# A fused attention and expert kernel: where the first routing runs, how token rows are turned, and when they are fetched

## The chip, the cores and the metric

The kernel runs on one core of one Trainium2 chip. A core has a matrix engine (TensorE, PE in the profile), a vector engine (VectorE, DVE), an activation engine (ScalarE, ACT), a general engine (GpSimd, POOL) and an engine that only issues transfers (SyncE, SP). They run side by side and wait for each other through semaphores. On-chip memory is SBUF, with 128 partitions; matmul results land in PSUM, eight banks of 512 fp32 columns in each partition. The metric is the device time in microseconds (us), the median of several runs.

## The reference: what is computed

Two stages. The first is attention with random features, over 8 batches, 8 heads, 576 positions, head dimension 64, 128 features:

```python
proj = np.einsum('bhsd,md->bhsm', x, omega)            # x is q or k
phi  = np.concatenate([np.cos(proj), np.sin(proj)], -1) / np.sqrt(m)
kv   = np.einsum('bhsm,bhsd->bhmd', k_p, v)
z    = np.sum(k_p, axis=2)
out  = (q_p @ kv) / (q_p @ z)
```

The result, as 4608 token rows of 512, goes through a mixture of 8 experts. Each token takes the one expert whose embedding has the largest cosine with the row; the gate is the softmax weight of that expert (temperature 0.1):

```python
expert_idx = np.argmax(xn @ en.T / tau, axis=1)
out[mask]  = gate_w[mask, None] * (np.maximum(x[mask] @ w1[e], 0) @ w2[e])
```

with w1 of 512 x 1024 and w2 of 1024 x 512 for each expert.

## The kernel before

**Attention.** There are 32 steps, one for each batch and pair of heads (heads i and i+4). The order of the instructions is written by hand (`manual_schedule`), as a software pipeline: pass n of the loop at L940 works on step n's keys and queries, on the projection of step n+1's keys, on the numerators of step n-1, and on the squares of steps n-2 and n-3. On PE a pass runs, in this order: `proj_q(n)` (L225, L232), `kv_turn(n-1)` (L308, L316), `proj_k(n+1)` (L213), `num(n-1)` (L341, 72 records), the transposes of raw k and q (`turns`, L180), `kv_products(n)` (L287). VectorE copies kv results out of PSUM (`kv_copy` L297, `kv_out` L326), takes the fraction of the angle (`frac`, L249), its absolute value for the cosine (`fold`, L255), the normalised output (`norm`, L356 to L358), and the sums of squares (L385). It also copies the turned keys, 640 columns, out of PSUM (`copy_k`, L191). ScalarE rounds the angles (`whole_turns`, L245), takes four sines a step (`wave`, L262), squares rows (L377) and copies the turned queries, 512 columns (`copy_q`, L200). GpSimd sums the key features for the denominator (`zsum`, L273 to L277, five additions for each of the two halves), casts the output to fp16 rows (L373), adds the logits (L407), and issues the cast loads of the expert weights (L92, L98).

The numerators wait for `kv_out`, which on VectorE stands behind whatever was put ahead of it in the pass; and `kv_turn` waits for `zsum`.

**Routing.** Tokens are sorted by expert into blocks of 128 rows, each of a single expert, so that a block is one dense product. The first half of the batches is routed during attention (`route_first`, passes 18 on): `choose` finds the expert of each token, `scan` and `rank` (two matmuls) its position within the expert, `places` and `places2` the block and row, `block_hot`, `row_hot` and `invert` the inverse: for each row of a block, its token. Only whole blocks of the first half are placed there; the first K1 = 11 blocks are safe to fetch before the second half is known. The rest is routed by `route_second`, during the first blocks of the expert stage. The gate needs the root of the sum of squares: Newton steps on VectorE for the first half (L693 to L716), `pow` on GpSimd for the second (L690).

**Experts.** The number of blocks is fixed: NBLK = 4608/128 + 8 - 1 = 43, the most that any split of the tokens can need. A block beyond those in use holds token numbers out of bounds, which gather and scatter skip. In iteration j PE runs `hidden(j+1)` (L840: 32 matmuls, weights stationary), the transposes of block j+2's rows (`turn_x`, L798: four of 128 x 128 in fp16, then a copy from PSUM at L792 or L790) and `result(j)` (L861: 8 matmuls of 512 columns). The rows are fetched with an indirect transfer into a ring of three buffers (`gather`, L759), five blocks ahead from iteration 0 on. The scaled result goes out with an indirect transfer (L874). The weights sit in SBUF, and the expert of a block is read into a PE register (`expert_of`); 40 further registers hold the addresses of its weight tiles (`place`).

Of the kernel before, what the change touches and what calls it, by code (L numbers as in the profile page):

```python
# [28 lines left out]
def kernel(  # L29
# [43 lines left out]

    ident = persist.tile([P, P], FP32)
    ident16 = persist.tile([P, P], FP16)
    sltb = persist.tile([P, P], BF16)
    onesb = persist.tile([P, P], BF16)

    w1_sb = persist.tile([P, E, 4, 1024], FP16)
    w2_sb = persist.tile([P, E, 8, 512], FP16)  # L80
# [5 lines left out]
    W1BASE, W2BASE = 18046, 83328  # L86
# [28 lines left out]
    eblk = persist.tile([1, NBLK], I32)  # L115
# [3 lines left out]
    io_k = io_p[:, 0:NBLK]  # L119
    io_kf = persist.tile([1, NBLK], FP32)  # L120
    pref = persist.tile([P, E], BF16)
    tri = persist.tile([P, E, E], FP32)
    sm = persist.tile([P, 12, E], FP32)
    zmask = persist.tile([P, 2], FP32)
    pio2 = persist.tile([P, 1], FP32)
    sel = persist.tile([P, SG, E], BF16)
    pm = persist.tile([P, SG], BF16)
# [4 lines left out]
    with tc.tile_pool(name="psA", bufs=1, space=PSUM) as psA, tc.tile_pool(  # L132
# [6 lines left out]

        steps = [(b, i) for b in range(B) for i in range(NPAIR)]  # L140
# [5 lines left out]
        def load(n, t, src):  # L146
            b, i = steps[n]
            for hh in range(2):
                nc.sync.dma_start(
                    out=t[64 * hh : 64 * hh + 64],  # L150
                    in_=src[b, i + 4 * hh].rearrange("(p c) d -> p c d", c=NCH),
                )

        raw = {}


        def load_kq(m):
            if m == -2:
                raw[m] = w1_sb[:, E - 2].rearrange("p c f -> p (c f)").bitcast(FP32)[:, 0 : NCH * 64]
                load(0, raw[m].rearrange("p (c d) -> p c d", d=64), k)  # L160
                return
            t = pa.tile([P, 2 * NCH, 64], FP32, tag="kq", name="kq", bufs=1)
            load(min(m + 2, NS - 1), t[:, 0:NCH], k)
            if m + 1 >= 0:
                load(m + 1, t[:, NCH:], q)
# [22 lines left out]
        def copy_k(m):  # L188
            t = pa.tile([P, 5 * P], FP32, tag="kT", name="kT", bufs=1)
            if m + 1 >= 0:  # L190
                nc.vector.tensor_copy(t, qreg[:, 0 : 5 * P])  # L191
                st.setdefault(m + 1, {})["t"] = t
            else:
                nc.vector.tensor_copy(t[:, 0 : 4 * P], qreg[:, 0 : 4 * P])  # L194
                nc.vector.tensor_copy(t[0:64, 4 * P :], qreg[0:64, 4 * P : 5 * P])
            st.setdefault(m + 2, {})["kT"] = t

        def copy_q(m):
            t = pa.tile([P, 4 * P], FP32, tag="qT", name="qT", bufs=1)
            nc.scalar.activation(t, qreg[:, 5 * P :], AF.Copy)  # L200
            st[m + 1]["qT"] = t

# [4 lines left out]
        def proj_k(n):  # L207
            t = st[n]["kT"]
            for j in range(5):
                for par in range(2 if j < 4 else 1):  # L210
# [4 lines left out]
                        lhsT=t[r0 : r0 + 64, j * P : j * P + P],  # L215
# [5 lines left out]
        def proj_q(n):  # L221
            d = st[n]
            for par in range(2):
# [4 lines left out]
                    rhs=d["qT"][r0 : r0 + 64],  # L228
                    start=True,
                    stop=True,  # L230
                )
            nc.tensor.matmul(  # L232
                qreg[:, 1024:1152],
                lhsT=omT[64:P],
                rhs=d["t"][64:P, 4 * P :],
# [30 lines left out]
        def zsum(n, half):  # L266
# [5 lines left out]
            zt = pa.tile([P, 2, P], FP32, tag="zt", name="zt", bufs=1)  # L272
            nc.gpsimd.tensor_tensor(zt, t[:, 0:2], t[:, 2:4], ALU.add)  # L273
            nc.gpsimd.tensor_tensor(zt, zt, t[:, 4:6], ALU.add)  # L274
            nc.gpsimd.tensor_tensor(zt, zt, t[:, 6:8], ALU.add)  # L275
# [73 lines left out]
        def norm(n):  # L349
# [3 lines left out]
            rd = pa.tile([P, 2, 5], FP32, tag="rd", name="rd")  # L353
# [15 lines left out]
        def to_rows(n):  # L369
# [3 lines left out]
            nc.gpsimd.tensor_copy(xrow[b, i // 2][:, :, i % 2], st[n]["xa"][:, 0:NCH, 0:64])  # L373

        def squares(n):
            x = st[n]["xa"][:, 0:NCH, 0:64]
            nc.scalar.activation(x, x, AF.Square)  # L377
# [11 lines left out]
        def square_rows(g):  # L389
            s0 = g * SG  # L390
            for par in range(2):
# [3 lines left out]
                nc.vector.tensor_copy(t[here, :, NPAIR:], t[there, :, 0:NPAIR])  # L395
                nc.vector.tensor_reduce(
# [3 lines left out]
        def sums(n):  # L400
            b, i = steps[n]
            src = st[n]["xa"][:, 0:NCH, 64 : 64 + E]
            if i == 0:
                lacc[b] = pa.tile([P, NCH, E], FP32, tag="la", name="la", bufs=3)
# [24 lines left out]
        emb_n = persist.tile([P, 2], FP32)  # L429
        load_kq(-2)  # L430
        for a in range(2):
            nc.scalar.dma_start(out=om2[:, a], in_=omega[:])
        nc.scalar.dma_start(out=emb, in_=moe_expert_emb[:])
        load_kq(-1)
        load_v(0)
        make_identity(nc, ident)
        nc.vector.memset(zmask, 0.0)
        nc.vector.memset(pio2, PI_2)
        nc.vector.memset(zmask[0:64, 0:1], 1.0)
# [15 lines left out]
        nc.gpsimd.memset(keep[:, :, 0:1], 0.0)  # L455
        nc.scalar.activation(
            emb2[:, :, 0], emb.rearrange("p (h d) -> p h d", d=64), AF.Square, accum_out=emb_n[:E, 0:1]
        )
        nc.scalar.activation(emb_n[:E, 0:1], emb_n[:E, 0:1], AF.Sqrt)
        nc.scalar.preload_act_table_set("silu_and_others")  # L460
        nc.vector.memset(nm2[:, 1, 4 * W : 5 * W], 1.0)
        tp_om = kreg[:, 0:P]
# [3 lines left out]
        copy_k(-2)  # L466
        proj_k(0)
# [9 lines left out]
        frac(0, "k")  # L477
        copy_k(-1)
        copy_q(-1)
        load_kq(0)  # L480
        tp_e = ps[:, 6 * 512 : 6 * 512 + H * E]
        for h in range(H):
# [4 lines left out]
            )  # L487

# [41 lines left out]
        def choose(g):  # L530
# [4 lines left out]
            nc.vector.tensor_copy(l0, a0[64:P])  # L535
            nc.vector.tensor_copy(l1, a1[0:64])
            nc.vector.tensor_tensor(l0, l0, a0[0:64], ALU.add)
            nc.vector.tensor_tensor(l1, l1, a1[64:P], ALU.add)
            mx = lmax[:, s0 : s0 + SG]
            nc.vector.tensor_reduce(mx, lg, axis=AX.X, op=ALU.max)  # L540
            nc.vector.tensor_tensor(sel, lg, bc(mx, [P, SG, E], 2), ALU.is_equal)
            nc.vector.tensor_tensor(sel, sel, bc(pref, [P, SG, E], 1), ALU.mult)
# [594 lines left out]
```

## Time and profile before

| | us |
|---|---|
| median of 3 runs | 520.08 |
| lowest and highest | 517.64, 525.76 |
| span of the profiled execution | 527.1 |

| group (line) | count | busy us | mean ns |
|---|---|---|---|
| first expert product, PE (L840) | 1376 | 83.7 | 219 |
| second expert product, PE (L861) | 344 | 81.3 | 379 |
| numerators, PE (L341) | 2304 | 160.9 | 235 |
| transposes of token rows, PE (L798) | 172 | 16.8 | 219 |
| copy of turned keys, VectorE (L191) | 32 | 26.3 | 821 |
| copy of turned queries, ScalarE (L200) | 32 | 19.1 | 598 |
| copy of turned token rows, VectorE (L792) | 35 | 14.8 | 424 |
| `choose`, last operation, VectorE (L544) | 4 | 2.6 | 662 |

Matmuls are pipelined, so the mean of one is its latency and not the time it adds. The first matmuls of the expert stage start at 340.25 us, so the stages take roughly two thirds and one third of the span.

### The profile page before, as it was taken

What the parts mean: (1) busy time and instruction counts of PE and PEld (TensorE: products, weight loads), DVE (VectorE), ACT (ScalarE), POOL (GpSimd) and SP (SyncE); (2) the same over time, 40 slices, a digit from 0 to 9 for tenths busy, and PEclk for the clock granted to TensorE, in tenths of its full rate; (3) what the DMA queues carried; (4) which work ended last, traced back from release to release, by engine and by line L of the source; (5) the groups of instructions that cost most, each with busy time, mean ns of one, the idle gap of its engine ahead of it and who ended that gap; (6) DMA issues with size and microseconds to landing.
All of it is one profiled execution on the core that took longest, in us unless ns stands there. A gap on an engine that the chain in (4) does not pass through costs nothing.

```text
span 527.1 us, 18983 instructions
## 1 busy us (share of the span) xinstructions
PE 480.5 (91%) x8012; PEld 397.2 (75%) x8012; DVE 353.1 (67%) x634; ACT 318.1 (60%) x375; POOL 377.8 (72%) x529
## 2 busy tenths in 40 slices
PE   5899999889999989999997989778989999999993
PEld 4798888779888878888886878666757776767771
DVE  4588787798788799999799899569613323232320
ACT  4678878676887885886686767644533332323331
POOL 2689999796999897989987688864545455554532
PEclk9799999999999999999899899999999999999998
DMA  4467778866698786687686774543223222223110
GB/s 114 120 149 160 170 161 176 162 132 132 158 183 149 167 173 132 154 176 146 129 186 119 156 137 100 106 95 82 91 92 106 97 68 103 95 93 104 56 52 0
DMA packets 57891, 65.61 MB, mean 124 GB/s; under 512 B 29637, under 2 KB 37829, under 8 KB 57808
## 3 DMA queue, kind: packets, MB, share of 16 engines
q0 software_dynamic: 18304, 30.97, 28.8%
q1 hardware_dynamic: 39200, 33.36, 25.4%
q8 instruction: 64, 1.05, 0.8%
q14 instruction: 19, 0.16, 0.1%
q10 hardware_dynamic: 304, 0.08, 0.1%
HBM read 67.90 MB, written 16.01 MB: 159 GB/s over the span
## 4 chain that ended last, share of the span: by engine, by line
PE 45%; POOL 21%; DVE 15%; ACT 8%; issue 7%; DMA 1%; POOLq 0%; ACTq 0%; SPq 0%; DVEq 0%
PE ps L840 12%; PE ps L861 10%; PE ps L341 8%; PE ps L287 4%; PE ps L180 4%; POOL zt L273 4%; POOL zs L276 3%; POOL zt L275 3%; POOL zt L274 3%; PE ps L213 3%; POOL zs L277 3%; PE ps L798 2%; ACT siq L245 2%; DVE cok L255 2%; ACT sik L262 2%
## 5 line engine op out<-in xcount | busy, mean ns | idle before, releaser
L840 PEld LDWEIGHTS <-w_sb 128*128 x1376 | 80.2, 98 | 21.0 <-issue 15.4
L341 PE MATMUL ps<-kv,siq 128*64 128x73 f32 x1152 | 81.1, 236 | 15.0 <-DVE kv L326 14.3
L840 PE MATMUL ps<-kq,w_sb 128*128 128x128 f16 x1376 | 83.7, 219 | 6.3 <-ACT kq L790 3.4
L852 DVE TENSOR_SCALAR cok<-ps 128x512 f16<-128x512 f32 x34 | 23.5, 692 | 88.1 <-PE ps L798 61.5
L341 PEld LDWEIGHTS ps<-kv,siq 128*64 128x64 f32 x1152 | 67.2, 142 | 19.5 <-ACT sik L245 8.1
L861 PE MATMUL ps<-w_sb,cok 128*128 x344 | 81.3, 379 | 0.1
L341 PE MATMUL ps<-kv,coq 128*64 128x73 f32 x1152 | 79.8, 233 | 0.0
L341 PEld LDWEIGHTS ps<-kv,coq 128*64 128x64 f32 x1152 | 67.8, 143 | 0.0
L200 ACT ACTIVATE qT<-ps 128x512 f32<-128x512 f32 x32 | 19.1, 598 | 68.2 <-DVE kT L191 64.6
L759 POOL DMA_INDIRECT xin_all<-rf_x,prm x43 | 46.7, 1086 | 15.1 <-issue 7.0
L861 PEld LDWEIGHTS <-cok 128*128 128x128 f16 x344 | 31.9, 98 | 31.0 <-issue 0.5
L249 DVE SCALAR_TENSOR_TENSOR sik<-sik,ps 128x1152 f32<-128x1152 f32 x32 | 43.2, 1350 | 6.7 <-ACT sik L245 6.7
L874 POOL DMA_INDIRECT out_dram<-sik,prm x22 | 22.1, 1006 | 35.2 <-ACT sik L873 35.0
L213 PE MATMUL ps<-omT,kT 64*128 64x128 f32 x576 | 46.2, 292 | 0.6 <-DVE kT L194 0.6
L273 POOL TENSOR_TENSOR zt<-sik 128x256 f32<-128x256 f32 x32 | 23.9, 747 | 31.8 <-ACT sik L262 31.5
L874 POOL DMA_INDIRECT out_dram<-siq,prm x21 | 21.6, 1026 | 34.4 <-ACT siq L873 32.6
L276 POOL TENSOR_TENSOR zs<-zt 128x128 f32<-128x128 f32 x64 | 41.4, 646 | 5.0
L249 DVE SCALAR_TENSOR_TENSOR siq<-siq,ps 128x1152 f32<-128x1152 f32 x32 | 43.0, 1344 | 2.2 <-ACT siq L245 2.1
L213 PEld LDWEIGHTS ps<-omT,kT 64*128 64x128 f32 x576 | 40.1, 196 | 2.1 <-DVE kT L194 1.0
L873 ACT ACTIVATE sik<-ps,gpos 128x512 f32<-128x512 f32 x22 | 15.1, 688 | 43.6 <-PE ps L861 43.6
L180 PE MATMUL ps<-ident,kq 128*128 128x128 f32 x288 | 40.2, 287 | 0.9 <-DVE siq L249 0.9
L245 ACT ACTIVATE sik<-ps 128x1152 f32<-128x1152 f32 x32 | 36.2, 1131 | 7.6 <-PE ps L213 7.2
(220 smaller groups left out, 1263.2 us busy)
## 6 DMA issues: line engine op xcount, KB each, us to landing
w_sb<-in_moe_w_dram POOLq DMA_DIRECT2D x32, 512.0 KB
kq<-in_k_dram SPq DMA_DIRECT2D x64, 144.0 KB, 3.4
kq<-in_q_dram SPq DMA_DIRECT2D x64, 144.0 KB, 3.4
v<-in_v_dram SPq DMA_DIRECT2D x34, 144.0 KB, 2.9
rf_x<-xb SPq DMA_DIRECT2D x32, 144.0 KB, 7.4
xin_all<-in_v_dram SPq DMA_DIRECT2D x30, 144.0 KB, 3.3
xin_all<-rf_x,prm POOLq DMA_INDIRECT x43
out_dram<-sik,prm POOLq DMA_INDIRECT x22
```

The costliest lines, as they stand in the source:

```text
L180: nc.tensor.transpose(qreg[:, j * P : j * P + P], t[:, j * P : j * P + P], ident)
L213: nc.tensor.matmul(kreg[:, s * P : s * P + P], lhsT=t[r0 : r0 + 64, j * P : j * P + P], rhs=omT[r0 : r0 + 64], start=True, stop=True,)
L245: nc.scalar.activation(si, REG[nm], AF.Copy, bias=CMAGIC, scale=1.0)
L249: nc.vector.scalar_tensor_tensor(out=si, in0=si, scalar=CMAGIC, in1=REG[nm], op0=ALU.subtract, op1=ALU.subtract)
L273: nc.gpsimd.tensor_tensor(zt, t[:, 0:2], t[:, 2:4], ALU.add)
L276: nc.gpsimd.tensor_tensor(z, zt[:, 0], zt[:, 1], ALU.add)
L341: nc.tensor.matmul(nm2[r0 : r0 + 64, a, (c - c0) * W : (c - c0) * W + W], lhsT=ph[:, s * P + r0 : s * P + r0 + 64], rhs=d["kv"][:, half, h ...
L759: ins = nc.gpsimd.indirect_dma_start(out=t, out_offset=None, in_=x_rows[:], in_offset=bass.IndirectOffsetOnAxis(ap=prm[:, j : j + 1], axis=0),
L840: nc.tensor.matmul(h_ps[:, f * P : f * P + P], lhsT=weights(k), rhs=d["xT"][:, c * P : c * P + P], start=(c == 0), stop=(c == 3),)
L852: nc.vector.tensor_scalar(hT[:, 512:], h_ps[:, 512:], 0.0, None, ALU.max)
L861: nc.tensor.matmul(y_ps, lhsT=d["hT"][:, c * P : c * P + P], rhs=weights(NW1 + c), start=(c == 0), stop=(c == NW2 - 1),)
L874: ins = nc.gpsimd.indirect_dma_start(out=out[:], out_offset=bass.IndirectOffsetOnAxis(ap=prm[:, j : j + 1], axis=0), in_=y, in_offset=None ...
```

## The change

The same computation with many small edits. The parts:

- **First routing.** Its VectorE operations are no longer issued where they stand: they are held in a list and released, up to a budget of estimated time (0.9 us) ahead of `kv_out`, and the rest after it. The work is cut into smaller pieces over more passes (18 to 31). Its scratch memory and the gates are reused in place. The root is `pow` on GpSimd, three columns at a time.
- **Split copies.** The keys' copy takes 512 columns and the queries' copy 640, so that each reads PSUM banks of its own; in 13 passes ScalarE does both.
- **Token rows.** Blocks 3 to 39 are turned by a DMA transpose issued from SyncE, straight from SBUF to SBUF, three blocks ahead. Blocks 0 to 2 keep the PE transposes.
- **Expert words.** The experts of eight blocks are packed into a word of three-bit digits; PE loads one word for eight blocks and takes digits out with register operations.
- **Gather.** Rows are fetched four blocks ahead instead of five.
- **Last blocks.** Blocks 40 to 42 stand under a condition on the number of blocks in use; the scatters of blocks 38 and 39 come after it.
- **Start.** Loads are spread over two queues, table loads are reordered with a root on GpSimd, filler matmuls keep TensorE busy, and the key features are summed with four additions instead of five. PE's instructions are aligned to 128 at one place in each of passes 1 to 20.

The diff, cut to its core:

```diff
         def load(n, t, src, second=nc.sync):
...
+        rv, ra = Engine(nc.vector), Engine(nc.scalar)
+
+        def release(budget):
+            spent = 0.0
+            while held:
...
+                cost = 0.2 + width / 960.0
+                if spent + cost / 2 > budget:
+                    return
...
         def copy_k(m):
-            t = pa.tile([P, 5 * P], FP32, tag="kT", name="kT", bufs=1)
+            t = pa.tile([P, 4 * P], FP32, tag="kT", name="kT", bufs=1)
+            if m in ROUTED:
+                nc.scalar.activation(t, qreg[:, 0 : 4 * P], AF.Copy)
+            else:
+                nc.vector.tensor_copy(t, qreg[:, 0 : 4 * P])
...
-            nc.scalar.activation(t, qreg[:, 5 * P :], AF.Copy)
+                nc.scalar.activation(t, qreg[:, 4 * P :], AF.Copy)
...
-            zt = pa.tile([P, 2, P], FP32, tag="zt", name="zt", bufs=1)
-            nc.gpsimd.tensor_tensor(zt, t[:, 0:2], t[:, 2:4], ALU.add)
-            nc.gpsimd.tensor_tensor(zt, zt, t[:, 4:6], ALU.add)
-            nc.gpsimd.tensor_tensor(zt, zt, t[:, 6:8], ALU.add)
+            zt = pa.tile([P, 4, P], FP32, tag="zt", name="zt", bufs=1)
+            nc.gpsimd.tensor_tensor(zt, t[:, 0:4], t[:, 4:8], ALU.add)
+            nc.gpsimd.tensor_tensor(zt[:, 0:2], zt[:, 0:2], zt[:, 2:4], ALU.add)
...
-        nc.scalar.activation(emb_n[:E, 0:1], emb_n[:E, 0:1], AF.Sqrt)
-        nc.scalar.preload_act_table_set("silu_and_others")
+        nc.gpsimd.tensor_tensor(emb_n[:E, 0:1], emb_n[:E, 0:1], emb_n[:E, 1:2], ALU.pow)
...
+        keep_warm(8)
...
+        def root(a, b):
+            nc.gpsimd.tensor_tensor(
+                lsq[:, a:b, E], lsq[:, a:b, E], half.to_broadcast([P, b - a]), ALU.pow
+            )
...
+        def turn_x_dma(j):
+            xT = late("kq", j % 4, 512)
+            nc.sync.dma_start_transpose(
+                out=xT.rearrange("p (c t) -> p c t", c=4), in_=xin[j][:, 0:D].bitcast(FP16)
+            )
+            mo[j] = {"xT": xT}
...
         def expert_of(j):
...
+            if w not in words:
+                word_of(w)
+            r = eoff[j % 2]
+            if k < 2:
+                nc.tensor.reg_alu(r, words[w], 6 - 3 * k, ALU.logical_shift_left)
+            else:
+                nc.tensor.reg_alu(r, words[w], 3 * k - 6, ALU.logical_shift_right)
+            nc.tensor.reg_alu(r, r, (E - 1) * EXB, ALU.bitwise_and)
...
+            if 0 < n <= n1 + 2:
+                nc.tensor.addr_align(128, STEP_AT)
...
+            hold[0] = True
+            route_first(n)
+            hold[0] = False
+            release(0.9 if n < NS - 1 else 0.0)
             if n == NS:
-                expert_of(0)
-                expert_of(1)
-                place(0, range(NW1 + NW2))
                 hidden(0, "act")
...
                 kv_turn(n - 1)
                 kv_out(n - 1)
+            release(100.0)
...
-        for j in range(NBLK):
-            eng = "act" if j <= QUIET else "dve"
...
+        def block(j, end):
+            if j + 1 < end:
+                hidden(j + 1, "act")
             route_second_pe(j)
+            if j < end - 2:
+                turn_x(j + 2, "act")
+            if 3 < j + 3 < LAST:
+                turn_x_dma(j + 3)
             route_second(j)
+            if j + 4 < NBLK:
+                gather(j + 4)
...
             result(j)
+            if not LAST - 2 <= j < LAST:
+                scatter(j)
+
+        for j in range(LAST):
+            block(j, LAST)
+        late("coq", 0, 2 * D)
+        nb = nc.values_load(nblk[0:1, 0:1], min_val=N // P, max_val=NBLK,
+            skip_runtime_bounds_check_because="counts of compares with E starts")
+        with tc.If(nb > LAST):
...
+            for j in range(LAST, NBLK):
+                block(j, NBLK)
+        scatter(LAST - 2)
+        scatter(LAST - 1)
```

## The prediction

> **What bounds the kernel now.** I read the page first, then stretches of the span, the chain of waits, the waits themselves, and the last 35 us in order of time. The page's busy row:
> ```profile
> PE 480.5 (91%) x8012; PEld 397.2 (75%) x8012; DVE 353.1 (67%) x634; ACT 318.1 (60%) x375; POOL 377.8 (72%) x529
> ```
> TensorE leads, but two stages hide in that average. By stretches (PE, weight load, DVE, ACT, POOL, clock, DMA):
> ```profile
> 60.00:80.00 20.00, 19.84 (x402) 17.20 (x393) 16.29 (x25) 16.51 (x18) 18.45 (x29) 1.00 0.80 170
> 200.00:220.00 20.00, 18.87 (x383) 16.82 (x382) 19.53 (x34) 15.33 (x16) 16.00 (x24) 1.00 0.77 159
> 280.00:300.00 20.00, 18.01 (x334) 16.13 (x331) 18.42 (x33) 11.72 (x14) 15.04 (x23) 0.91 0.57 116
> 440.00:460.00 20.00, 20.00 (x234) 14.63 (x233) 5.88 (x15) 6.79 (x11) 10.30 (x10) 1.00 0.28 93
> ```
> Attention without routing is PE-bound (19.84 of 20), with GpSimd close behind at 18.45. Once routing of the first half runs (from about 195 us), VectorE is at 19.5 and PE loses time. The expert stage is PE alone. Steps show in the chain of waits, at the start of the 72 numerator matmuls:
> ```profile
> 64.22 2.44 PE ps L341 x72
> 83.15 2.45 PE ps L341 x72
> ...
> 97.36 1.90 issue
> ...
> 289.97 4.14 PE ps L341 x72
> 301.66 2.51 PE ps L341 x72
> ```
> Two clean steps take 83.15 - 64.22 = 18.93, so 9.47 each; the routed one 11.69. 97.36 is PE waiting for nothing that the profile shows. 4.14 against 2.44 is the matmuls at half clock. The mechanism, in one step of the chain:
> ```profile
> 114.86 0.78 DVE eq L544
> 115.63 0.30 DVE kv L326
> ...
> 116.07 4.14 PE ps L341 x72
> ```
> The last operation of `choose` (L544) stands ahead of `kv_out` (L326) on VectorE, and PE waits for `kv_out`. Two rows of the waits:
> ```profile
> ACT qT L200 <- DVE kT L191: 64.6, 31, 5.2
> PE ps L341 <- DVE kv L326: 14.3, 13, 2.1
> ```
> ScalarE idles 2.1 us a step until VectorE has copied kT. Last, the expert stage in order of time: PE alone, then VectorE's copy of the turned rows, then the end by stretches:
> ```profile
> 501.91 1.95 PE L840 MATMUL ps<-kq,w_sb 128*128 128x128 f16 x32
> 503.69 0.39 PE L798 MATMUL ps<-ident,xin_all 128*128 128x128 f16 x4
> 503.92 1.89 PE L861 MATMUL ps<-w_sb,cok 128*128 x8
> 505.75 1.95 PE L840 MATMUL ps<-kq,w_sb 128*128 128x128 f16 x32
> ```
> ```profile
> 505.27 0.42 DVE L792 COPY kq<-ps 128x512 f16<-128x512 f16 x1 [0.63 <-PE ps L798]
> ```
> ```profile
> 512.00:516.00 4.00, 4.00 (x44) 2.79 (x43) 1.77 (x4) 1.28 (x2) 0.98 (x1) 1.00 0.02 1
> 516.00:520.00 4.00, 2.62 (x13) 0.98 (x10) 0.00 (x0) 1.37 (x2) 1.35 (x2) 1.00 0.02 0
> ```
> A block takes 505.75 - 501.91 = 3.84, elsewhere up to 3.88: 1.79 hidden, 0.22 transposes, 1.83 to 1.89 until the next hidden, which starts 0.06 after the copy ends (505.69): PE waits for it. From 512 us on almost nothing moves (1 and 0 GB/s) though blocks 40 to 42 are still computed and scattered.
>
> **What the Trainium skill says.** "TensorE: Matmul & The Clock Gate", "Wait — 56ns, not 53.3ns?": 55.6 ns between matmuls of 128 columns, 215.7 of 512. The trace agrees: 1.79/32 = 56 ns. So a block with transposes costs at least 36 x 0.0556 + 8 x 0.2157 = 3.73, without them 3.51 (estimates). The same page, "Part 1: The HAM clock gate": the clock is halved until about 3.4 us of sustained work. It agrees: the first 20 us have a mean clock of 0.84, and 4.14 follows an idle of 2.07. "PSUM — Partial Sum Buffer", "PSUM bank collisions": two engines may not touch one bank at once. That fits the 64.6: kT's 640 columns and qT's 512 share a bank; 512 and 640 don't. "DMA: Bandwidth & Descriptors", "Latency and other measured facts": a DMA transpose moves 261 GB/s or more, with 600 ns to the first byte; no DMA transpose is in this trace.
>
> **The change, part by part.**
>
> Skipped blocks: the inputs of the reference give expert counts 1155, 712, 0, 1151, 438, 576, 574, 2 (worked out from it), so 10+6+0+9+4+5+5+1 = 40 blocks of 128; 40 is LAST, and the guarded three don't run. The zero GB/s above says the same. After: PE ends with block 39's result, without hidden(40) and its transposes ahead of it. Before, result 39 ended at 509.49 and PE at 518.63: 9.14 + 1.79 + 0.22 = 11.2 us less. The guard costs a register load and a branch per engine, and scatters 38 and 39 stand behind it. Nothing like a branch is in the trace; PE's stop of 1.62 us ahead of the first hidden (two register loads and 72 adds) is the nearest row. 0 to 3, I take 1.5.
>
> Transposes by DMA: 37 of 40 blocks lose 0.22 on PE, 8.2 us, and the copy (0.42 DVE or 0.60 ACT) that PE waits for: 3.87 against 3.73, so 0.14 x 37 = 5.2, of which I take 5 (0 if the sequencer is the cause). That leaves 3.51 to 3.65 per block. In exchange gather, transpose and hidden form a chain: gather(j+4) starts about 2.6 us after hidden(j+1) (496.77 against 494.15), I allow 3 to land, and the rows are needed three blocks later, at 10.5. That leaves 4.9 us for the transpose. By the skill 0.6 + 131 KB/261 GB/s = 1.1 us; the nearest rows are the 144 KB loads of q (3.4 to landing) and the stores in short pieces (7.4). I take 3.4: hidden. At 7.4 a block would take (2.6 + 3 + 7.4)/3 = 4.3. Behind a waiting transpose SP queues only more transposes and the stores of the second half.
>
> Packed words: one load per 8 blocks in place of one each. But hidden(40) and hidden(41), with loads of words beside them, started 3.74 and 3.73 before the next (505.75, 509.49, 513.22), the price of the matmuls alone. So I count nothing.
>
> Stalls early in the expert stage: hidden(1) at 346.45 to 518.63 is 172.2; 43 blocks by 3.87 less the first hidden, plus 1.6 for rank and inversion, is 166, so 6 us of stalls, mostly hidden behind xT copies on ACT. Those go from block 3 on. But VectorE's second routing isn't shorter (27 us busy from 340 to 380), while PE arrives some 4 us earlier at the inversion of block 6. I keep 4 of 6: 2 us less. Gathers one block later have slack for it.
>
> Routing of the first half: the ops stay about as many (Newton's 13 small ones go to GpSimd as `pow`; its one row is 3.27 us for 18 columns, so 0.5 for 3), but before `kv_out` only some 0.9 us of them may run; the rest follow it, beside the numerators on PE. The kT copy of 13 steps (0.82) moves to ACT, so VectorE drops to about 7.4 + 2 us of routing in 9.45. ACT then has 1.12 + 1.13 + 2 x 1.16 + 2 x 1.25 + 0.70 + 0.60 + 0.68 = 9.05: close to its limit, but freed of the wait of 2.1. GpSimd: two sums of 3 x 0.735 + 2 x 0.46 become 1.28 (512 wide, from the slope of the 128 and 256 rows) + 0.735 + 2 x 0.46, 0.2 less each. Address alignment aims at fetch stops such as 97.36; about 1 us in all. Before, the 31 gaps from kvT at 22.2 to 338.7 average 10.21. After, I take 17 at 9.4 and 14 at 9.75, sum 296.3 against 316.5: 20 us less. Best case, all at 9.3: 28. Worst, routed steps stay at 10.4: 11.
>
> Start: two of three table loads (1.28 each) go, loads are shared between two queues, and filler matmuls open the clock. The first step ended at 22.2; half clock cost kv products 2.84 against 2.2, transposes 2.18 against 1.13, k projections 2.50 against 1.31. 3.5 us less (1 to 5). The registers of blocks 0 and 1 are set earlier, at the seam: 1 of 1.62 us.
>
> Memset, constants, buffers made aliases, one gate store for two, gate ops in place: off the path, nothing. Weight pieces issue elsewhere in GpSimd's same cycle: nothing.
>
> Sum: -11.2 + 1.5 - 8.2 - 5 - 2 - 20 - 3.5 - 1 = -49.4; 520.1 - 49.4 = 471.
>
> **The rivals.** (a) ACT becomes the bound of the routed steps: 9.05 busy in order, with waits on VectorE's folds inside. Routed steps stay at 10.4 and the second routing stalls PE as before: 9 + 2 more, and 2 of fetch stops, 484. For it: ACT's 96%; against: its idle of 2.1 goes. (b) All goes well: steps at 9.3, no stalls: 8 + 4 less, 458. (c) The transpose takes 7.4: 36 blocks at 4.3 instead of 3.51 give 28 more, 500. (d) The transpose is far slower than any row here, say 12 us and so 5.9 per block: 86 more, about 555, slower than before. Only the lack of any such row speaks for it.
>
> **How the numbers follow.** Forecast 0.55, (a) 0.20, (b) 0.13, (c) 0.06, (d) 0.04; 0.02 for a new queue stall that eats everything (within 2%). From 455 to 496 holds the forecast, (a) and (b) and leaves out (c), (d) and the rest, with a little of (b). Faster 0.94, same 0.02, slower 0.04.
>
> **What would show it.** No matmuls of L798's kind after block 2, and hidden and result together at 3.5 to 3.65 us; 40 results; no wait of PE for a DMA transpose; ACT's wait for kT gone; numerators starting every 9.3 to 9.8 us between 195 and 320; half clock gone after the first 8 us; the first hidden near 316. Wrong if PE waits on the transposes' landing, if routed steps stay over 10.3, or if the branch costs over 4 us at the end.

## The result and the profile after

| | before | after |
|---|---|---|
| median of 4 runs, us | 522.75 | 478.20 |
| lowest to highest | 517.64 to 525.76 | 475.16 to 484.07 |
| span of the profiled execution | 527.1 | 473.3 |

The ratio of the times is 0.9197, with a 95% interval from 0.9095 to 0.9299; it is taken from the fast runs alone, those within 1.5% of their kernel's fastest, whose means are 518.86 before and 477.19 after. The forecast was 471, the range 455 to 496.

The page's busy row (engine, busy us, share of the span, instructions):

```profile
PE 453.8 (96%) x7778; PEld 379.9 (80%) x7778; DVE 295.7 (62%) x523; ACT 345.9 (73%) x439; POOL 366.9 (78%) x472
```

TensorE is busy for 27 us less, but its idle time, span less busy, went from 46.6 to 19.5 us as well. VectorE lost 57 us; ScalarE gained 28. The stretches of attention and of the experts, in the columns of before (length, then PE, weight load, DVE, ACT, POOL, then clock, DMA share and GB/s):

```profile
60.00:80.00 20.00, 20.00 (x429) 17.95 (x430) 16.17 (x25) 17.34 (x19) 17.66 (x24) 1.00 0.90 163
200.00:220.00 20.00, 19.93 (x424) 17.82 (x422) 18.52 (x34) 18.32 (x20) 18.29 (x24) 1.00 0.79 159
280.00:300.00 20.00, 20.00 (x427) 17.98 (x428) 18.63 (x34) 18.27 (x20) 17.68 (x24) 1.00 0.73 136
440.00:460.00 20.00, 20.00 (x224) 14.32 (x222) 0.00 (x0) 10.97 (x24) 11.92 (x12) 1.00 0.49 125
```

The third row is where the change shows most: from 280 to 300 us PE had 18.01 of 20 and a clock of 0.91; now it is full at full clock, while VectorE is still at 18.6. GpSimd, at 18.45 in the first row before, is at 17.66. In the last row VectorE has no work left at all.

The chain of waits, at the start of the numerators, and the two rows of waits that stand where the old ones stood (engine and line, what it waited for, us in all, times, longest):

```profile
60.00 2.44 PE ps L389 x72
69.23 2.44 PE ps L389 x72
78.46 2.44 PE ps L389 x72
```
```profile
DVE kv L374 <- PE ps L364: 17.0, 17, 2.2
ACT qT L246 <- PE ps L227: 11.6, 17, 1.2
```

A clean step is 78.46 - 69.23 = 9.23, where it was 9.47. VectorE now waits for PE's `kv_turn` to copy `kv_out`, as it should when PE is the bound, and ScalarE's copy of the queries waits for PE's transposes, 1.2 us at most, where it waited 64.6 us for VectorE's copy of the keys. The expert stage in order of time:

```profile
456.05 1.95 PE L926 MATMUL ps<-kq,w_sb 128*128 128x128 f16 x32
457.83 1.89 PE L947 MATMUL ps<-w_sb,cok 128*128 x8
459.56 1.95 PE L926 MATMUL ps<-kq,w_sb 128*128 128x128 f16 x32
461.35 3.62 PE L947 MATMUL ps<-w_sb,cok 128*128 x16
```

A block is 459.56 - 456.05 = 3.51, against 3.84 to 3.88. The last `hidden` is followed by two results, and PE is done at 464.97; no block beyond the fortieth runs. The transposes appear among the transfers (how many, median us to landing) and in one row of PE's waits:

```profile
kq<-xin_all SPq DMA_TRANSPOSE x37, 3.3
```
```profile
PE ps L926 <- DMA kq<-xin_all: 1.0, 2, 0.8
```

They take 3.3 us from issue to landing, and PE waited for them twice, for 1.0 us in all.

### The profile page after: what moved, and what is told of

It reads as the page before. It is cut to its first block, busy times and chain, and to the rows that moved or that the text cites. A ratio compares the mean times of both kernels' runs of the same rounds, so it can differ in the third digit from the quotient of the medians.

```text
span 473.3 us, 18511 instructions
## 1 busy us (share of the span) xinstructions
PE 453.8 (96%) x7778; PEld 379.9 (80%) x7778; DVE 295.7 (62%) x523; ACT 345.9 (73%) x439; POOL 366.9 (78%) x472
## 3 DMA queue, kind: packets, MB, share of 16 engines
q1 hardware_dynamic: 59168, 37.80, 33.5%
## 4 chain that ended last, share of the span: by engine, by line
PE 49%; POOL 20%; issue 15%; DVE 6%; DMA 6%; ACT 2%; POOLq 1%; ACTq 0%
PE ps L389 13%; PE ps L335 10%; POOL xin_all L821 7%; PE ps L261 6%; PE ps L227 6%; PE ps L273 5%; POOL out_dram L974 3%; DMA out_dram<-sik,prm 3%; POOL zt L322 3%; PE ps L364 2%; PE ps L356 2%; DMA kq<-in_q_dram 2%; PE ps L926 2%; POOL zs L324 2%; POOL zt L323 2%
## 5 line engine op out<-in xcount | busy, mean ns | idle before, releaser
L926 PE MATMUL ps<-kq,w_sb 128*128 128x128 f16 x1280 | 78.0, 219 | 2.1 <-DMA kq<-xin_all 1.0
L947 PE MATMUL ps<-w_sb,cok 128*128 x320 | 75.4, 379 | 0.5 <-issue 0.5
L821 POOL DMA_INDIRECT xin_all<-rf_x,prm x43 | 45.9, 1067 | 13.6 <-issue 13.0
L322 POOL TENSOR_TENSOR zt<-sik 128x512 f32<-128x512 f32 x32 | 41.1, 1284 | 19.7 <-ACT sik L311 19.4
L323 POOL TENSOR_TENSOR zt<-zt 128x256 f32<-128x256 f32 x64 | 48.5, 758 | 5.0
L294 ACT ACTIVATE siq<-ps 128x1152 f32<-128x1152 f32 x32 | 36.2, 1130 | 16.0 <-PE ps L281 15.9
L322 POOL TENSOR_TENSOR zt<-cok 128x512 f32<-128x512 f32 x32 | 43.4, 1356 | 0.0
L311 ACT ACTIVATE siq<-siq 128x1152 f32<-128x1152 f32 x32 | 37.1, 1158 | 6.4 <-DVE coq L304 6.4
L311 ACT ACTIVATE cok<-cok,consts 128x1152 f32<-128x1152 f32 x32 | 39.9, 1246 | 0.0
L311 ACT ACTIVATE coq<-coq,consts 128x1152 f32<-128x1152 f32 x32 | 39.8, 1244 | 0.0
L311 ACT ACTIVATE sik<-sik 128x1152 f32<-128x1152 f32 x32 | 37.0, 1156 | 1.5 <-DVE cok L304 1.5
```

Of the source, the lines that this page charges most:

```text
L294: nc.scalar.activation(si, REG[nm], AF.Copy, bias=CMAGIC, scale=1.0)
L311: nc.scalar.activation(t, t, AF.Sin, bias=pio2 if which == "co" else 0.0, scale=-TWO_PI * SINSC)
L322: nc.gpsimd.tensor_tensor(zt, t[:, 0:4], t[:, 4:8], ALU.add)
L323: nc.gpsimd.tensor_tensor(zt[:, 0:2], zt[:, 0:2], zt[:, 2:4], ALU.add)
L821: ins = nc.gpsimd.indirect_dma_start(out=t, out_offset=None, in_=x_rows[:], in_offset=bass.IndirectOffsetOnAxis(ap=prm[:, j : j + 1], axis=0),
L926: nc.tensor.matmul(h_ps[:, f * P : f * P + P], lhsT=weights(k), rhs=d["xT"][:, c * P : c * P + P], start=(c == 0), stop=(c == 3),)
```

## Experiments

All ratios are to the kernel before, run on the same chip; the spans are to be held against 473.3. Most have two timed runs, so that their intervals overlap with that of the change; what follows rests on the part of the trace that each edit touches. A "step" below is the time from one copy of kv (L345) to the next.

**1. All 43 blocks, no condition.**
```diff
-        LAST = N // P + E // 2
+        LAST = NBLK
...
-        with tc.If(nb > LAST):
...
```


> The changed kernel without the condition: blocks 40 to 42 are always computed. Theory (the three blocks cost their matmuls, the condition almost nothing): TensorE ends 3 x 3.51 = 10.5 us later, the stretch from TensorE's last result to the end of the span stays at 8.3 us, so the span goes from 473 to about 484. Rival (the branch and the load ahead of it cost the 1.5 us that the prediction took, or more): that stretch shrinks by 1.5 to 3 us, and the span grows by 7.5 to 9 only.

Median 488.41, ratio 0.9382 [0.9204, 0.9560], span 488.4. From the second `hidden` to the end of PE it took 153.9 us, against 143.0: the three blocks cost 10.9. From there to the end of the span it took 8.9, against 8.3 with the condition. So the condition has no cost that shows. (Two attention steps of 11.63 and 10.86, which the edit doesn't touch, make most of the rest of its span; in each PE stopped, as told in experiment 7.)

**2. Token rows turned by TensorE again, their copies on VectorE from block 9 on.**
```diff
-        turn_x_dma(3)
...
             if j < end - 2:
-                turn_x(j + 2, "act")
-            if 3 < j + 3 < LAST:
-                turn_x_dma(j + 3)
+                turn_x(j + 2, "act" if j <= 7 else "dve")
```


> The changed kernel with all token rows turned on TensorE again; the copies out of PSUM on ScalarE up to block 9, on an otherwise idle VectorE from block 10 on. Theory (two costs in the kernel before: 0.22 us of transposes on TensorE, and 0.14 of waiting for a copy that stood behind a relu on VectorE): with VectorE free of the relu the copy ends in time, so late blocks take 3.73 us, not 3.87; 30 late blocks add 6.6 us, and the first ten another 3 to 6 through copies behind ScalarE's relus. Span about 484. Rival (the 0.14 belongs to the transposes themselves or to the sequencer): late blocks at 3.87, span about 489.

Median 482.93, ratio 0.9277 [0.9166, 0.9388], span 480.3. PE in order of time:
```profile
440.47 1.95 PE L926 MATMUL ps<-kq,w_sb 128*128 128x128 f16 x32
442.25 0.39 PE L870 MATMUL ps<-ident,xin_all 128*128 128x128 f16 x4
442.48 1.89 PE L947 MATMUL ps<-w_sb,cok 128*128 x8
444.20 1.95 PE L926 MATMUL ps<-kq,w_sb 128*128 128x128 f16 x32
```
A block is 3.73, the 3.51 and the 0.22 of the transposes. The 0.14 that the kernel before spent on top was therefore not theirs; it was the copy behind VectorE's other work, which here has gone. The trace of the kernel before says the same: in blocks 13 to 40 `hidden` starts 0.05 us after the end of that copy each time, and blocks 41 and 42, whose copy ended earlier, take 3.73 and 3.74. The stage is 150.2, 7.3 more. The early blocks, with copies on ScalarE, also ran at 3.74, but for one of 3.99 and one of 6.31 at the inversion: a few extra us that I expected there did not come.

**3. One word for each block.**
```diff
-    PACK = 8
+    PACK = 1
...
```


> The changed kernel with one expert word for each block (43 loads into registers of TensorE instead of 6). Theory (a load runs beside the queued matmuls): late blocks stay at 3.51 us, the span within 1 us of 473. Rival (the register load was the 0.14 us a block of the kernel before): 3.65 us a block, span about 479.

Median 485.17, ratio 0.9320 [0.9128, 0.9512], span 485.3. Undisturbed blocks take 3.513 as before: the loads are free. Its 12 us lie elsewhere: an attention step of 15.24, in which PE stopped for 4.12 us within one group of matmuls, one of 10.58, and three longer early blocks. Stops of that kind are taken up in experiment 7.

**4. Gather right ahead of its transpose, three blocks ahead.**
```diff
+            route_second(j)
+            if 3 < j + 3 < NBLK:
+                gather(j + 3)
             if 3 < j + 3 < LAST:
                 turn_x_dma(j + 3)
-            route_second(j)
-            if j + 4 < NBLK:
-                gather(j + 4)
```


> The changed kernel with each gather, and the DMA transpose behind it, one block later (three blocks ahead instead of four). Theory (a chain of 2.5 us to the gather's issue, 3.1 to its landing, 3.3 for the transpose, 9 us in all, against three blocks of 3.51 before the rows are needed; now only two): late blocks take 9/2 = 4.5 us, TensorE waits for the transposes' landing, span about 473 + 36 = 509. Rival (there is far more slack, since the landings overlap): blocks stay at 3.51 and the span at 473.

Median 511.03, ratio 0.9817 [0.9633, 1.0000], span 507.3. PE in order of time, and its wait:
```profile
447.31 1.89 PE L947 MATMUL ps<-w_sb,cok 128*128 x8
451.42 1.95 PE L926 MATMUL ps<-kq,w_sb 128*128 128x128 f16 x32 [2.22 <-DMA kq<-xin_all]
453.20 1.89 PE L947 MATMUL ps<-w_sb,cok 128*128 x8
```
```profile
PE ps L926 <- DMA kq<-xin_all: 30.0, 15, 3.0
```
Every third block waits. The stage is 176.5, 33.5 more: about 0.9 a block, and three quarters of what the change had won. One place in the order decides whether the chain of gather and transpose is hidden.

**5. The first routing issued where it stands.**
```diff
-            hold[0] = True
+            hold[0] = False
             route_first(n)
```


> The changed kernel with the first routing's VectorE operations issued where they stand, all ahead of the kv copy, instead of held to 0.9 us ahead of it and the rest behind. Theory (TensorE waits for the kv copy, and some 1 us more of routing now stands ahead of it in about 12 passes, half of it in slack): the 14 gaps of passes 16 to 30, 133.6 us in the changed kernel, grow by 6 to 10, the span to about 481. Rival (cutting the routing into small pieces and moving the keys' copy did it all): they stay within 2 us of 133.6.

Median 479.23, ratio 0.9172 [0.9056, 0.9289], span 478.9. The fourteen routed steps before the last sum to 138.2 against 133.6; the worst are 12.67 and 11.26, in passes with much routing ahead of `kv_out`. So the list is worth 4.6 us, less than the 6 to 10 I gave it. At the seam to the expert stage this kernel is 1.7 us shorter than the change, to which I come back.

**6. All copies of the keys on VectorE.**
```diff
-        ROUTED = tuple(range(n1, n1 + 13))
+        ROUTED = ()
```


> The changed kernel with the keys' copy on VectorE in all passes, also in the 13 with routing. Theory (VectorE is the engine without slack in those passes): 0.69 us more for it in each, about 0.4 of it seen, so the gaps of passes 16 to 30 grow by about 5 us from 133.6. Rival (ScalarE, 9.05 us busy in each of these passes, had become their bound): they get shorter by 1 to 3 us.

477.38 and 488.40, two runs so far apart that no ratio is given; span 475.5. The two routed stretches:
```profile
200.00:220.00 20.00, 18.93 (x376) 16.19 (x374) 19.72 (x35) 15.77 (x16) 17.29 (x24) 1.00 0.79 159
280.00:300.00 20.00, 19.66 (x406) 17.09 (x402) 19.66 (x33) 16.13 (x17) 17.27 (x24) 1.00 0.77 148
```
VectorE goes up to 19.7 and PE loses 1.0 and 0.3 of 20 us. The fourteen steps sum to 135.6, 2.0 more; 5 were expected. Experiments that don't touch these steps (1 to 4, 9 and 10) have sums from 133.5 to 135.5, so the 2.0 alone would prove little; that VectorE is fuller and PE emptier in both stretches is what speaks for it. Had ScalarE been the bound of the routed steps, taking these copies from it would have made them shorter.

**7. No alignment of PE's instructions.**
```diff
-            if 0 < n <= n1 + 2:
-                nc.tensor.addr_align(128, STEP_AT)
...
```


> The changed kernel without the alignment of TensorE's instructions. Theory (alignment only keeps stops for instructions away from bad places): the median of the first 16 gaps stays at 9.25, one or two stops of 1 to 2 us come back as in the kernel before (97.36), span about 475. Rival (it is the alignment that took the median from 9.48 to 9.25): 9.4 or more, span about 477.

Median 491.01, ratio 0.9398 [0.9211, 0.9585], span 485.7, 12 more where 2 were expected. Clean steps are 9.20 to 9.26, as with it; the time is in stops inside `kv_products`, in PE's order of time and its waits:
```profile
120.73 0.28 PE L335 MATMUL ps<-cok,xin_all 64*64 64x128 f32 x2
123.73 0.33 PE L335 MATMUL ps<-sik,xin_all 64*64 64x128 f32 x2 [2.72 <-issue]
```
```profile
PE ps L335 <- issue: 6.3, 3, 2.7
```
Both sides of the stop are matmuls of one group with the same inputs, so no data was late: PE's instruction stream stopped. Three such stops gave steps of 12.48, 12.46 and 11.11; after the first two TensorE ran at half clock for a while, and the next steps took 10.70 and 10.39. But stops of the same kind are in other profiles that have the alignment: 1.62 and 1.40 us in experiment 1, 4.12 and 1.10 in 3, 3.60 in 9, 3.27 in 10, 2.17 in 11; none in the change's own nor in the other six. The kernel before has the one of 1.90.

What these stops wait for can be read from the transfers. One DMA queue of the profile is called instruction; it moves packets of 16 KB, one every 4 to 10 us in attention (queue, kind: packets, MB, share of 16 engines; the change):
```profile
q8 instruction: 64, 1.05, 0.9%
```
Each of these eleven stops ends 1.2 to 1.6 us after such a packet has landed. Here the packets land at 122.18, 201.35 and 223.36, and PE goes on at 123.73, 202.77 and 224.91; in experiment 3 it is 123.37 and 124.72. This fits PE waiting for instructions that came late, and nothing else in the traces fits all eleven; why a packet comes late the runs don't show. With the alignment the stops always fall after 26 or 27 of the 72 matmuls of `kv_products`, without it after 40 and 45.

Three stops in the one profile without the alignment, against none to two in each of the twelve with it, suggest that it makes them rarer; it doesn't end them. Which of the 12 us belongs to the alignment, and which to one execution's luck, one profile can't tell.

**8. Five additions in the sum of the features.**
```diff
-            nc.gpsimd.tensor_tensor(zt, t[:, 0:4], t[:, 4:8], ALU.add)
-            nc.gpsimd.tensor_tensor(zt[:, 0:2], zt[:, 0:2], zt[:, 2:4], ALU.add)
+            nc.gpsimd.tensor_tensor(zt, t[:, 0:2], t[:, 2:4], ALU.add)
+            nc.gpsimd.tensor_tensor(zt, zt, t[:, 4:6], ALU.add)
+            nc.gpsimd.tensor_tensor(zt, zt, t[:, 6:8], ALU.add)
...
```


> The changed kernel with five additions for the sum of the key features in place of four, as in the kernel before. Theory (the denominator's sum ends last before kv_turn, as the gaps of 0.3 us ahead of L316 in the kernel before show): 0.2 us more for each of two sums takes the median of the first 16 gaps from 9.25 back to about 9.45, span +6. Rival (GpSimd's sum is hidden): 9.25, span unchanged.

Median 487.81, ratio 0.9337 [0.9225, 0.9448], span 484.8. The clean stretch and a piece of the chain of waits:
```profile
60.00:80.00 20.00, 19.62 (x388) 17.38 (x390) 15.30 (x24) 16.72 (x18) 18.63 (x30) 1.00 0.81 168
```
```profile
71.28 0.73 POOL zt L322
...
72.08 0.74 POOL zt L323
...
72.90 0.75 POOL zt L324
...
73.72 0.47 POOL zs L325
```
The chain runs through GpSimd, and the median clean step is 9.46 again. So it does in the kernel before, where two matmuls of `kv_turn` stand between the end of the sum and the second of these lines:
```profile
60.89 1.06 POOL zs L276
...
62.91 1.31 PE ps L213 x18
```
In the change the chain of the same stretch is all PE. So the sum on GpSimd set the step of the kernel before, by a little, and the shorter sum gave 9.46 - 9.25 = 0.21 a step. In the fourteen routed steps it is worth 8.0 us (141.6 against 133.6). There PE waits visibly for the sum, 6.9 us in all against 1.1 in the change:
```profile
PE ps L365 <- POOL zs L326: 6.9, 11, 1.0
```

**9. VectorE's copy of the keys reaching 32 columns into the bank that ScalarE copies.**
```diff
-                nc.vector.tensor_copy(t, qreg[:, 0 : 4 * P])
+                nc.vector.tensor_copy(t, qreg[:, 0 : 4 * P + 32])
...
```


> The changed kernel with 32 columns more in VectorE's copy of the keys, unused, so that it reads the bank of the queries' copy again and ScalarE waits for it; in the 18 passes without routing. Theory (the wait of 64.6 us in the kernel before was hidden, since TensorE bounds these passes): the median of the first 16 gaps stays at 9.25, though ScalarE's wait for kT is back. Rival (the wait delays the queries' projection): 9.4 or more, span +3 to +5.

Median 482.28, ratio 0.9275 [0.9224, 0.9325], span 481.1. ScalarE's wait for VectorE's copy is back, which bears out the shared bank as its cause:
```profile
ACT qT L248 <- DVE kT L240: 28.3, 19, 2.7
```
The median of the first 16 steps is 9.37, between theory and rival. The first three steps are longer, 9.50 to 9.55, and one of 9.77; most other clean ones are 9.20 to 9.26, as in the change, though the wait is there too. A step of 13.76 with a stop of PE, and the 10.49 after it, make most of the span. The wait, 1.5 us each time, is nearly hidden. So the split of the copies is not where the time of the clean steps came from; the routed ones were not tried.

**10. No filler matmuls.**
```diff
-        keep_warm(8)
-        keep_warm(2)
-        keep_warm(5)
...
```


> The changed kernel without the filler matmuls at the start. Theory (they open TensorE's clock early and hold it): the first pass ends at 21.5 to 22 us instead of 19.5, with half clock after 10 us as in the kernel before. Rival (the spread loads and the table loads saved made the start shorter): it ends at 19.5 to 20.5.

Median 487.16, ratio 0.9368 [0.9294, 0.9443], span 487.5. PE's starts after an idle time:
```profile
20.41 2.15 PE L227 MATMUL ps<-ident,kq 128*128 128x128 f32 x9 [3.70 <-issue]
26.96 1.13 PE L273 MATMUL ps<-qT,omT 64*128 64x512 f32 x4 [1.65 <-DVE cok L304]
```
The same nine transposes in the change:
```profile
15.47 1.20 PE L227 MATMUL ps<-ident,kq 128*128 128x128 f32 x9 [0.41 <-DVE siq L298]
```
Half the clock and a stop of 3.70. The first copy of kv comes at 25.4 instead of 19.5, and the first step takes 10.96 instead of 9.26: 7.6 us in all, well over the forecast. Part of it is the clock, part the stop, which no engine's data explains and ahead of which no instruction packet lands either; one profile can't part them. The rest of the 14 us is one step of 15.11 with a stop.

**11. The choice of the third batch pair one pass later.**
```diff
             elif m == 13:
-                choose(GRP1)
                 square_rows(GRP1)
+            elif m == 14:
+                choose(GRP1)
                 choose2(GRP1)
```


> The changed kernel with the choice of experts of the third batch pair moved from pass 31, where 4 us of it stand ahead of the fraction of the angles, to pass 32, where VectorE sits idle for 3.5 us. Theory (this delay holds up the last queries' angles, the last kv copy and the normalisation, opens gaps on TensorE and so halves its clock twice, 3.4 us each): from pass 31's start to the second hidden 20.4 us become 16 to 17, one or both half-clock stretches go, span about 469. Rival (the first hidden, put ahead of kv_turn, and the register adds cause it): 20 us as now, span 473.

Median of 4 runs 477.22, ratio 0.9172 [0.9112, 0.9232], span 476.2. From the last but one copy of kv to the second `hidden` it takes 17.4 instead of 20.5, the direction of the theory, if not its 16 to 17; why is told below. The span of 469 did not come: in this profile the 3.1 us were lost again to a step of 12.86 with a stop of PE.

**12. Experiment 11, the words of the first experts three passes earlier, and the 48 register additions ahead of the expert stage spread over three passes.**
```diff
-            place(0, range(NW1 + NW2))
-            place(1, range(NW1 + NW2, NW1 + 2 * NW2))
+            for k in range(16 * part, 16 * part + 16):
+                place(0 if k < NW1 + NW2 else 1, [k])
...
```


> As the kernel before this in the list, and besides: the first experts' words are computed in pass 24 instead of 27, where a conversion of two numbers took 1.54 us on VectorE, and the 48 register adds for the first blocks are spread over the query projections of passes 29 to 31. Theory: the gap of 10.98 us at pass 27 becomes 9.5, the stop of 0.9 us in pass 31 goes, span about 466, time about 471. Rival (other work in those passes ends last anyway): no gain over the kernel before this in the list.

Median of 4 runs 474.80 (473.66 to 478.63), ratio 0.9146 [0.9083, 0.9210], span 473.3, the same as the change's; 466 was expected. The step that the moved words had lengthened is 9.25 instead of 10.98, but the next is 11.07 instead of 9.79, where other routing has taken their place. The seam is 18.0 instead of 20.5. A median 3.4 us below that of the change, with intervals that overlap, is no gain that these runs establish.

## Why the prediction was right, and where it was not

The sum, term by term, in the profiled executions (a gap is the time from one copy of kv to the next):

| step of the prediction | predicted | measured | from |
|---|---|---|---|
| skipped blocks | -11.2 | -10.9 | experiment 1 |
| their condition | +1.5 | 0 | PE's end to the span's end, 8.5 before, 8.3 after |
| transposes and the copy, 37 blocks | -13.2 | -13.0 | 37 x (3.865 - 3.513) |
| stalls early in the expert stage | -2 | -5.3 | stage 172.2 to 143.0, less the two rows of blocks |
| attention, 31 gaps | -20 | -21.3 | first to last kv copy, 316.5 to 295.2 |
| start | -3.5 | -2.7 | first kv copy, 22.2 to 19.5 |
| registers set earlier, at the seam | -1 | -0.4 | last kv copy to second `hidden`, 7.8 to 7.3 |

The kernel before was profiled in an execution of 529.0 us, 10.1 above the mean of 518.86 given with the result, so the measured column holds some 10 us that a usual execution of it doesn't have. The rows of the blocks repeat from block to block; for the early stalls, the attention and the start nobody can say how much of the excess is in them.

**Skipped blocks** came out as worked out from the counts. **The condition** was charged by the stop of 1.62 us ahead of the first `hidden`, which has register work of another size, and which itself ends 2.1 us after a packet of instructions landed; experiment 1 shows nothing of the kind. Nothing in the trace of before bore on it, and "Advanced Engine Details and Errata", "Control Flow Timing", in the Trainium skill, has some 108 ns for a compare and branch: I should have taken that end. Our runs agree as far as they can tell.

**Transposes and copy**: right, and for the reason given. The prices of the matmuls alone had given 3.51 and 3.73; the change and experiment 2 measure 3.513 and 3.737. The kernel before, at 3.865, had the copy on top. The transpose took 3.3 us to land, and 3.4 had been taken from the loads of q; that these two agree is luck, and the other estimate, 1.1 us, was a third of it. Experiment 4 shows that rivals (c) and (d) named the real danger: with the rows fetched one block, 3.5 us, later, against the reserve of 1.5 that I had worked out (4.9 less 3.4), every third block waits. The **packed words** do nothing, as said (experiment 3).

**Early stalls**: 5.3 of 6 went, and I kept four of the six because VectorE's second routing isn't shorter. The first blocks now take 3.5 to 3.9 us and only those at the inversion, 4.5 and 5.5, are longer. The DMA transposes aren't needed for that: experiment 2, with the rows turned on TensorE and copied by ScalarE, has hardly any such stalls. In the kernel before, `hidden` of blocks 4, 5, 7 and 9 starts 0.05 us after ScalarE's copy of the rows, and that copy stands behind a relu for which ScalarE had sat idle 0.8 to 2.3 us. What made that relu late, and which part of the change ended it, is open.

**Attention steps**: the total came out near, the mechanism only in part. I gave clean steps 9.4 and got 9.25; I had worked out that the sum on GpSimd would be 0.2 shorter for each half, and put it down to an engine near the bound, not to the bound. PE's 19.84 of 20 us had hidden that it waited. Experiment 8 shows that this sum was the bound of the clean steps, and worth some 11 us over all, the largest part that any experiment shows. In the routed steps 9.75 was expected and 133.6/14 = 9.54 measured. The mechanism that the forecast rested on, routing ahead of `kv_out`, is there, but smaller: the list with its budget gives 4.6 and the moved copies at most some 2 (experiments 5 and 6), the shorter sum 8.0 of these steps. That a part left small and a part taken too large made up for each other is luck. The cutting of the routing into smaller pieces and the root on GpSimd were not tried alone. ScalarE, at 18.3 of 20 us, doesn't bind (experiment 6), which is against rival (a). The split of the copies removed a wait of 64.6 us and hardly any time of the clean steps (experiment 9). The first thirty gaps became 25.0 us shorter in all; the last one, at the seam, took 3.8 back (9.39 to 13.15).

**Start**: right within 0.8, but not shown part by part. Without the fillers the first copy of kv comes 3.2 later than in the kernel before (25.4 against 22.2), and a stop of 3.70 without a known cause lies in that (experiment 10); so what fillers, loads and tables are each worth stays open.

**Seam**: by this I mean the stretch from the last but one copy of kv to the second `hidden`, in which the last gap of attention and the start of the expert stage lie over each other. The prediction had it a little shorter: the last gap at 9.75 for 9.39, and 1 off PE's stop of 1.62, through the registers of two blocks set earlier. It grew from 17.2 to 20.5. The stop did shrink; others came. PE in the last pass, starts after an idle time:

```profile
303.43 0.37 PE L281 MATMUL ps<-qT,omT 64*128 64x128 f32 x1 [0.90 <-issue]
305.50 0.35 PE L389 MATMUL ps<-kv,siq 128*64 128x73 f32 x4 [0.65 <-DVE kv L374]
312.31 1.95 PE L926 MATMUL ps<-kq,w_sb 128*128 128x128 f16 x32 [0.32 <-DVE siq L298]
315.16 0.67 PE L356 MATMUL ps<-rmat,kvT 64*128 64x72 f32 x8 [0.91 <-DVE kvT L345]
317.02 0.51 PE L389 MATMUL ps<-kv,siq 128*64 128x73 f32 x4 [0.65 <-ACT cok L934]
322.01 1.95 PE L926 MATMUL ps<-kq,w_sb 128*128 128x128 f16 x32 [0.69 <-ACT kq L852]
```

My theory after the result was that the choice of the third pair, released whole between `kv_out` and the fraction of the last queries (VectorE, 305.38 to 310.98), pushes everything behind it. Experiment 11 moves it away and 3.1 us go. But the idle times don't bear that out. They sum to 4.12 in the change; in the same stretch before there are stops of 0.65, 1.20, 1.62 and 0.65, also 4.12, and in experiment 11 0.39, 0.65, 1.69, 0.65 and 0.69, which is 4.07. Idle time was neither lost nor won. What differs is the clock. Short stretches of the change, with the clock in the third column from the end:

```profile
306.00:308.00 2.00, 2.00 (x48) 2.00 (x45) 1.87 (x6) 1.92 (x3) 1.64 (x2) 0.62 0.40 70
308.00:310.00 2.00, 2.00 (x33) 1.66 (x34) 1.85 (x6) 0.34 (x2) 1.84 (x4) 0.53 0.00 0
316.00:318.00 2.00, 1.35 (x20) 1.30 (x21) 1.12 (x2) 2.00 (x5) 1.34 (x2) 0.68 0.40 99
318.00:320.00 2.00, 2.00 (x39) 2.00 (x37) 0.00 (x0) 0.05 (x1) 0.00 (x0) 0.50 0.12 41
```

Two stretches of half clock, 3.4 us each, so 1.7 us lost in each. With the loss summed over windows of 1 us (one less the clock), length less idle less loss is nearly the same in every kernel:

| kernel | length | PE idle | clock loss | rest |
|---|---|---|---|---|
| before | 17.2 | 4.1 | 0 | 13.0 |
| the change | 20.5 | 4.1 | 3.4 | 12.9 |
| experiment 2 | 20.2 | 5.3 | 1.7 | 13.2 |
| experiment 5 | 18.8 | 4.0 | 1.7 | 13.1 |
| experiment 6 | 18.3 | 3.4 | 1.7 | 13.3 |
| experiment 11 | 17.4 | 4.1 | 0 | 13.3 |
| experiment 12 | 18.0 | 2.7 | 1.7 | 13.6 |

The other seven profiles have a clock loss of 3.4 (experiment 1) or 1.7 (3, 4, 7 to 10), and a rest of 12.8 to 13.3.

So the +3.3 is the clock, and the 1 us that was to come from the registers went to stops that took the place of the old one. In the Trainium skill, "TensorE: Matmul & The Clock Gate", "What's actually happening", has the gate watch a free-running window of some 3.4 us; stretches of 3.4 here agree, and so does it that the same idle time halves the clock in one kernel, or twice, and not at all in another. The idle time itself is much shorter than such a window: no stop in the list above is longer than 0.91. Whether the place of the choice matters to it, or only the phase of that window in one execution, a single trace of each kernel doesn't tell. It stays open. Experiment 12 has the choice moved too, and one halving.

**From span to time.** The profiles differ by 53.8 us and the medians by 44.6; the means that the ratio is taken from differ by 41.7. I took the terms from the profiled execution of before, 527.1 us of span and 529.0 of time, and subtracted their sum, 49.4, from the median, 520.1. That execution is longer than all four timed ones of its kernel (517.64 to 525.76), and that of the change is the shortest of its four. Stops of PE such as those of experiment 7 are one thing in which the profiles differ. On the profiles the sum was 4.4 too cautious; on the means it asked for 7.7 too much. That is why 478 and not 471 is measured though most terms came out larger than forecast.

## What to carry to other kernels

When one engine is at 19.8 of 20 us, look at the next one behind it: what set the clean step was GpSimd, at 18.5, with a chain of dependent additions, and a wait of 64.6 us on ScalarE set hardly anything. The transposes by DMA cost TensorE 1.0 us of waiting in all while the fetch ahead of them was early enough, and moving that fetch about one block later took most of the gain back. Where a stretch grows, take idle time and clock loss apart before blaming a wait, and take a difference of a few us from several runs, not from one profiled execution; see first where that execution lies among the others. A stop inside a group of matmuls that no engine explains is worth holding against the times at which instructions land.

## What the runs showed of the hardware

- The clock at the seam: 0.90 + 0.65 us of stops within 3 us were followed by half clock for 3.4 us in the change; a single stop of 1.62 us in the kernel before and one of 1.69 in experiment 11 were not. In all fourteen profiles the loss at the seam is 0, 1.7 or 3.4 us, with nothing between.
- A small VectorE operation can take ten times its time next to a GpSimd one. In the change the cast of two numbers and what follows it, in VectorE's order of time, and GpSimd's at that moment:

```profile
266.37 1.54 DVE L177 CAST eblk<-w_sb 1x2 int32<-1x2 f32 x1
267.83 1.33 DVE L298 SCALAR_TENSOR_TENSOR siq<-siq,ps 128x1152 f32<-128x1152 f32 x1
```
```profile
266.59 1.29 POOL L322 TENSOR_TENSOR zt<-sik 128x512 f32<-128x512 f32 x1
```

  It ends with the GpSimd addition, at 267.9. In all twelve profiles in which this cast meets an addition (the change and experiments 1 to 11) it ends 0.02 to 0.04 us after it and takes 0.57 to 1.54; in experiment 12, at a place with no addition, it takes 0.16. The step around it, 10.98 us in the change, is no shorter where the cast takes 0.57 (11.84), so the cast isn't what makes it long.
- Stops of TensorE of 1.1 to 4.1 us in the middle of `kv_products`, eleven in seven of fourteen profiles, each ending 1.2 to 1.6 us after a packet of 16 KB landed on the queue called instruction (experiment 7).
